# A Hedgehog-attention and MoE kernel: a new issue order with smaller first MoE blocks, 64-row tiles for the q products, and results on VectorE

One core of a Trainium2 chip. The metric is device time in microseconds (us) of one execution, the median over several.

## The reference

Linear attention with a learned feature map, then a layer norm and a two-layer channel network ("MoE") with a residual. Shapes: 8 batches, 8 heads, 576 tokens, 64 columns per head; model width 512, hidden width 2048.

```python
def phi(x):                                    # x: (8, 8, 576, 64)
    proj = einsum('bhsd,df->bhsf', x, w_phi)   # f = 128
    proj = proj - max(abs(proj), axis=-1, keepdims=True)
    return concatenate([exp(proj), exp(-proj)], axis=-1)
q_p, k_p = phi(q), phi(k)
kv  = einsum('bhsf,bhsd->bhfd', k_p, v);  z = sum(k_p, axis=2)
att = einsum('bhsf,bhfd->bhsd', q_p, kv) / (einsum('bhsf,bhf->bhs', q_p, z)[..., None] + 1e-06)
x   = att.transpose(0, 2, 1, 3).reshape(8, 576, 512)
xn  = (x - mean(x)) / sqrt(var(x) + 1e-06) * g_ln
out = x + maximum(xn @ w_ch1, 0.0) @ w_ch2
```

## The kernel before

It works on pairs of batches. A "unit" is two sequences of 576 tokens (one head of both batches of a pair; in the first pair, two heads of one batch), so there are 32 units. Each operation is registered with an engine, an estimated duration, a rank and what it reads and writes; a list scheduler in the source then fixes one order of instructions per engine. Each engine gets its instructions in that order; the traces below show instructions held up behind one that waits (3.53 us on ScalarE in the first new dent). From unit 8 on q and k are cast to bf16 by any of three engines and transposed by DMA, before that on TensorE. Fillers are matmuls on zeros, meant to keep TensorE's clock up.

In the profile lines PE is TensorE (PEld its weight loads), DVE VectorE, ACT ScalarE, POOL GpSimd and SPq the queue that issues most DMAs. A timeline line gives start and duration in us; brackets hold the engine's idle time before it and what ended that.

```python
DUE = 24.7; BLOCK = 127.5; WARM = 45.0
...
b16_bufs = [consts.tile([P, ST], BF16, name=f"b16_{i}") for i in range(2)]   # cast q, k
...
def a_trans_dma(u):
    b16 = b16_bufs[n % 2]            # cast (DVE, ACT or GpSimd) -> b16 -> DMA transpose -> qkT
...
def a_main(u, i):                    # i = 0: q, i = 1: k
    for c in range(4):               # full rows, a zero-padded block weight: two heads at once
        nc.tensor.matmul(ps[:, 2 * c : 2 * c + 2, :],
            u["qkT"][:, (i * 4 + c) * P : (i * 4 + c + 1) * P], wbk, start=True, stop=True)
...
def a_tails(u):                      # q products, transposed
    for i in range(2):
        nc.tensor.matmul(ps[:, i * 512 : (i + 1) * 512], wbk[:, i, :], u["qkT"][:, 0:512],
                         start=True, stop=True)
...
# MoE: blocks of three token tiles (384 columns) for xn @ w_ch1, then 512 columns per tile for w_ch2
def result(engine):                  # (DVE, ACT): on ACT in 26 of 36 cases
    nc.scalar.activation(o, ch[t], AF.Copy, scale=pr["rstd"][:, t : t + 1])
def residual():
    nc.gpsimd.tensor_tensor(out=ch["o", t], in0=ch["o", t], in1=x[:, t, :], op=ALU.add)
```

## Time and profile before

| | before |
|---|---|
| time, median of 3 | 389.92 us (389.59 to 390.96) |
| span of the profiled run | 388.8 us |
| TensorE busy | 364.6 us, 94% |
| first MoE matmul | 49.13 us |
| last matmul ends, then tail | 382.8 us, 6.0 us |

"Busy" here includes fillers and waits inside a pipelined group, so the share says little. The prediction below shows the lines and turns them into a ledger of useful and lost TensorE time.

### The profile page before, as it was taken

How to read it: one execution, taken by the hardware profiler on the slowest of the kernel's cores; microseconds unless marked ns; L12 is line 12 of the kernel's file. 1: busy time of each engine (PE TensorE's matmuls, PEld its weight loads, DVE VectorE, ACT ScalarE, POOL GpSimd, SP SyncE). 2: the span in 40 equal slices, each digit the busy share in tenths (PEclk: the TensorE clock that was granted, in tenths of full speed). 3: DMA queues.
4: the chain of work that ended last, by engine and by line, in shares of the span. 5: the costliest groups of instructions: out<-in, count | busy, mean ns of one | idle time of the engine just before them, and what ended most of it. 6: DMA issues, size and time to landing. Idle time of an engine off the chain costs nothing.

```text
span 388.8 us, 8917 instructions
## 1 busy us (share of the span) xinstructions
PE 364.6 (94%) x3307; PEld 232.5 (60%) x3354; DVE 255.0 (66%) x556; ACT 259.8 (67%) x576; POOL 201.9 (52%) x348
## 2 busy tenths in 40 slices
PE   3999995999999989999999999999999999999993
PEld 1888864666766554666666556666665555555541
DVE  3788995899999999997897998696757000000000
ACT  2877885899786857797976887686946444444411
POOL 3667987577576836664936655935841111111022
PEclk9999998799999999999999999999999999999998
DMA  7999889979799284948861486220007030110012
GB/s 208 300 227 279 262 150 170 222 189 254 197 245 232 64 230 111 236 129 190 183 186 36 124 163 157 57 60 2 30 27 137 31 90 29 27 56 27 30 66 71
DMA packets 92444, 53.28 MB, mean 137 GB/s; under 512 B 58992, under 2 KB 87792, under 8 KB 92400
## 3 DMA queue, kind: packets, MB, share of 16 engines
q1 hardware_dynamic: 86400, 47.79, 48.8%
q0 software_dynamic: 4224, 4.19, 6.9%
q10 hardware_dynamic: 1776, 0.72, 0.7%
q8 instruction: 26, 0.43, 0.5%
q14 instruction: 18, 0.15, 0.1%
HBM read 36.77 MB, written 9.44 MB: 119 GB/s over the span
## 4 chain that ended last, share of the span: by engine, by line
PE 57%; issue 21%; DVE 11%; DMA 6%; POOL 3%; ACT 1%; POOLq 0%; SPq 0%; DVEq 0%
PE hT_ps L1006 20%; PE ch_ps L1037 16%; PE pm L624 6%; DMA qkT_130<-b_0_131 4%; PE n_bank L734 3%; POOL o L1056 3%; PE num L780 3%; PE n_bank L1215 2%; PE pt L699 2%; DVE m_137 L631 1%; DVE m_135 L631 1%; DMA qx_106<-in_k_dram 1%; DVE w_120 L451 1%; DVE st_147 L933 1%; PE n_bank L729 1%
## 5 line engine op out<-in xcount | busy, mean ns | idle before, releaser
L1037 PE MATMUL ch_ps<-w_121,hT 128*128 128x512 bf16 x541 | 145.3, 379 | 1.6
L1006 PEld LDWEIGHTS <-w_120 128*128 128x128 bf16 x768 | 72.7, 98 | 55.9 <-issue 2.5
L1016 ACT ACTIVATE hT<-hT_ps 128x384 bf16<-128x384 f32 x113 | 55.6, 493 | 59.4 <-PE hT_ps L1006 58.9
L1037 PEld LDWEIGHTS <-hT 128*128 128x128 bf16 x576 | 53.3, 98 | 43.8
L820 POOL TENSOR_TENSOR x<-numc,rden 128x384 bf16<-128x384 f32 (+3 forms) x88 | 46.2, 541 | 62.4 <-DVE rden L814 58.2
L1056 POOL TENSOR_TENSOR o<-o,x 128x512 f32<-128x512 f32 x26 | 30.1, 1157 | 85.9 <-ACT o L1050 80.5
L1006 PE MATMUL hT_ps<-xT_127,w_120 128*128 128x384 bf16 x256 | 52.0, 326 | 0.1
L1006 PE MATMUL hT_ps<-xT_125,w_120 128*128 128x384 bf16 x256 | 50.2, 329 | 1.4 <-DVE hT L1014 0.9
L1006 PE MATMUL hT_ps<-xT_126,w_120 128*128 128x384 bf16 x256 | 51.2, 326 | 0.1
L1014 DVE TENSOR_SCALAR hT<-hT_ps 128x384 bf16<-128x384 f32 x79 | 42.9, 549 | 9.8 <-PE hT_ps L1006 9.2
L643 ACT ACTIVATE eb_134<-pm 128x1024 bf16<-128x1024 f32 x32 | 32.8, 1036 | 3.5 <-DVE m_137 L631 1.5
L643 ACT ACTIVATE eb_133<-pm 128x1024 bf16<-128x1024 f32 x32 | 31.7, 1025 | 4.9 <-DVE m_137 L631 3.8
L705 ACT ACTIVATE ea_118<-pt 128x1024 bf16<-128x1024 f32 x32 | 31.9, 1032 | 4.0 <-PE pt L699 2.4
L705 ACT ACTIVATE ea_116<-pt 128x1024 bf16<-128x1024 f32 x32 | 31.5, 1028 | 4.2 <-PE num L786 1.5
L631 DVE TENSOR_REDUCE m_136<-pm 128x8 f32<-128x1024 f32 x22 | 26.6, 1215 | 6.4 <-PE pm L624 6.3
L631 DVE TENSOR_REDUCE m_135<-pm 128x8 f32<-128x1024 f32 x22 | 26.7, 1215 | 4.0 <-PE pm L624 4.0
L1045 DVE SCALAR_TENSOR_TENSOR o<-ch_ps,rstd_157,x 128x512 f32<-128x512 f32 x2 | 1.5, 752 | 41.4 <-PE ch_ps L1037 41.4
L631 DVE TENSOR_REDUCE m_137<-pm 128x8 f32<-128x1024 f32 x20 | 24.3, 1214 | 2.1 <-PE pm L624 2.1
L1215 PE MATMUL n_bank<-wz 128*128 128x120 bf16 x301 | 22.4, 221 | 1.6 <-DVE KV L742 1.0
L804 DVE TENSOR_TENSOR numc<-num,em 128x390 f32<-128x390 f32 (+1 forms) x40 | 20.3, 515 | 4.6 <-PE num L780 4.4
L810 DVE TENSOR_TENSOR numc<-numc,num 128x390 f32<-128x390 f32 (+1 forms) x40 | 20.4, 515 | 0.7
L1215 PEld LDWEIGHTS <-wz 128*128 128x128 bf16 x301 | 18.6, 101 | 3.1 <-issue 2.1
(204 smaller groups left out, 649.5 us busy)
## 6 DMA issues: line engine op xcount, KB each, us to landing
out_dram<-o SPq DMA_DIRECT2D x32, 256.0 KB, 2.5
qk_100<-in_k_dram SPq DMA_DIRECT2D x12, 256.0 KB, 3.8
v_101<-in_v_dram SPq DMA_DIRECT2D x12, 256.0 KB, 3.7
qk_102<-in_k_dram SPq DMA_DIRECT2D x10, 256.0 KB, 3.4
qk_102<-in_q_dram SPq DMA_DIRECT2D x10, 256.0 KB, 4.1
v_103<-in_v_dram SPq DMA_DIRECT2D x10, 256.0 KB, 4.6
qk_104<-in_k_dram SPq DMA_DIRECT2D x10, 256.0 KB, 4.0
qk_104<-in_q_dram SPq DMA_DIRECT2D x10, 256.0 KB, 4.7
```

What stands on the lines that cost most here:

```text
L624: nc.tensor.matmul(ps[:, 2 * c : 2 * c + 2, :], u["qkT"][:, (i * 4 + c) * P : (i * 4 + c + 1) * P], wbk, start=True, stop=True,)
L631: nc.vector.reduce_max(out=u["m"][:, i, 0:MX], in_=u["pm", i], axis=AX.X, apply_absolute_value=True)
L643: nc.scalar.activation(u["EB"][:, t, 0:MX, :], u["pm", 1], AF.Exp, scale=(1.0, -1.0)[t])
L705: nc.scalar.activation(u["EA"][:, t, 0:1024], u["pt"], AF.Exp, scale=(1.0, -1.0)[t])
L810: nc.vector.tensor_add(out=st["numc"], in0=st["numc"], in1=st["ps"][0])
L820: nc.gpsimd.tensor_tensor(out=dst, in0=st["numc"][ps_, i : i + n, 0:D], in1=bcast(st["rden"][ps_, i : i + n], 2, D), op=ALU.mult,)
L1006: nc.tensor.matmul(st["ps"], w1_sb[:, kc, jj * P : (jj + 1) * P], xT_bufs[(pair * NR + r) % XB][:, kc::KC, :], start=(kc == 0), stop=(kc = ...
L1014: nc.vector.tensor_relu(h_sb, st["ps"])
L1016: nc.scalar.activation(h_sb, st["ps"], AF.Relu)
L1037: nc.tensor.matmul(ch[t], hT[r, jj][:, rt * P : (rt + 1) * P], w2_sb[:, jj, :], start=(jj == 0), stop=(jj == JC - 1),)
L1056: nc.gpsimd.tensor_tensor(out=ch["o", t], in0=ch["o", t], in1=x[:, t, :], op=ALU.add)
L1215: nc.tensor.matmul(warm, wz, wz[:, 0:WN], start=False, stop=False, skip_group_check=True)
```

## The change

The intent: start the MoE sooner, so that fillers give way to useful work; halve the cost of q's products; shorten the tail; model the DMA rings in the scheduler so that no transposed data comes late. The scheduler and the ranks are rewritten, and with them every engine's order. The core, cut:

```diff
-DUE = 24.7
-BLOCK = 127.5
-WARM = 45.0
+DUE, SLOPE = 33.0, 1.3
+WARM = 36.0
+OFF = ( {"en": 0, "gln": 404.4, "k": 731.6, ... "mixed": 18.6, ...}, ... )   # new ranks [cut]
...
+    # MoE blocks in token tiles: the first pair of batches in 2, 2, 2 and 3, the others in 3
+    BLOCKS = (((0, 2), (2, 4), (4, 6), (6, 9)), *(((0, 3), (3, 6), (6, 9)),) * (NPAIR - 1))
...
+    # units 0 to 3: k and v of four units are loaded first, q is done in two halves (s = 0, 1) [cut]
...
+    def a_qt(u):                                # units 4 to 31: q and transposed q in one group
+        rows = [slice(a * D, (a + 1) * D) for a in range(2)]
+        for c in range(4):
+            for a in range(2):
+                nc.tensor.matmul(pq[:, a, c, :], qT[rows[a], c * P : (c + 1) * P],
+                                 wst[rows[a], :], start=True, stop=True)
+        for a in range(2):
+            nc.tensor.matmul(pt[:, a * 512 : (a + 1) * 512], wst[rows[a], :],
+                             qT[rows[a], 0:512], start=True, stop=True)
...
-            def result(engine):   # DVE, or ACT with the residual on GpSimd
+            def result():
+                nc.vector.scalar_tensor_tensor(
+                    out=o[:, cols], in0=ch[t, c][:, cols], scalar=pr["rstd"][:, t : t + 1],
+                    in1=x[:, t, cols], op0=ALU.mult, op1=ALU.add)   # the last tile in two halves
```

What it leaves alone matters too: there are still two cast buffers (`b16_bufs`).

## The prediction

> **What bounds the kernel now.** I read the page's shares first, then the busy table by stretches of the span, then TensorE's timeline, the chain of waits, and TensorE's groups by shape. TensorE is busy 94% of the span; nothing else passes 67%. The question is how much of that is useful.
>
> ```profile
> PE 364.6 (94%) x3307; PEld 232.5 (60%) x3354; DVE 255.0 (66%) x556; ACT 259.8 (67%) x576; POOL 201.9 (52%) x348
> PE   3999995999999989999999999999999999999993
> PEclk9999998799999999999999999999999999999998
> ```
>
> The tenths show a slow start, one dent near slices 6 and 7 (60 to 75 us) with a lower clock, and a full row from there to the end. The table (stretch in us, then mean length, busy us of PE, PEld, DVE, ACT, POOL, clock, DMA) sizes the parts:
>
> ```profile
> 5.00:10.00 5.00, 2.56 (x13) 1.27 (x14) 2.57 (x5) 2.57 (x4) 0.00 (x0) 1.00 1.08 290
> 60.00:70.00 10.00, 5.76 (x67) 4.05 (x68) 5.99 (x12) 4.92 (x8) 5.59 (x16) 0.77 1.26 188
> 120.00:140.00 20.00, 18.18 (x166) 11.13 (x168) 19.69 (x37) 14.30 (x31) 12.30 (x19) 1.00 0.65 180
> 320.00:340.00 20.00, 19.89 (x108) 10.59 (x109) 0.75 (x1) 8.92 (x18) 2.31 (x2) 1.00 0.09 27
> ```
>
> Up to 49 us TensorE is "busy" with fillers: matmuls on a zero tile that only keep its clock up. The first MoE matmul (L1006) starts at 49.13. The dent is a wait for one transposing DMA, issued at 52.16 and landed 15.38 us later, while the second weight's four loads (issued from 51.05 on) are in the rings:
>
> ```profile
> L1215 PE MATMUL n_bank<-wz 128*128 128x120 bf16 x301 | 22.4, 221 | 1.6 <-DVE KV L742 1.0 <-ACT KV L744 0.5
> 49.13 0.81 PE L1006 MATMUL hT_ps<-xT_125,w_120 128*128 128x384 bf16 x4
> 51.05 2.30 POOL L435 DMA_DIRECT2D w_121<-in_moe_w_ch_dram  x3
> 52.16 15.38 DMA qkT_130<-b_0_131
> 67.59 1.03 PE L624 MATMUL pm<-wbk,qkT_130 128*128 128x256 bf16 x4 [3.71 <-DMA qkT_130<-b_0_131]
> ```
>
> Durations of overlapped matmuls are no cost, so I take the distance between starts. 16 matmuls of 384 columns stand in the chain as 2.60 us, 0.1625 each; 9 of 512 columns as 1.94, 0.2157 each. The MoE is 768 and 576 of these (541 of the latter are recorded): 124.8 + 124.2 = 249.0 us. One attention unit, from the starts in the timeline: key products 0.44 (35.03 to 35.47), query products 0.44, transposed query products 0.43 (61.58 to 62.01), mixed tail 0.16, kv 2 x 0.31, numerators 0.37 + 0.25: 2.71 us, times 32 = 86.7. Transposes of the first eight units 8 x 0.5 = 4, of x 36 x 0.056 = 2. **Useful work: 341.7 us.** The last matmul ends near 382.8, so 41 us of TensorE's time is lost. A ledger by stretch finds it: fillers 301 at 0.053 to 0.107, about 17.5; idle in the first 10 us 6.5; half clock for useful work until 13 us, about 2.5; idle from 10 to 50 us 1.9; from 50 to 70 us 5.2; half clock after the dent about 2; idle from 70 to 160 us 3.0; from 160 to 380 us 1.6. Sum 40.2. So the time is useful work, plus what is lost before and around the MoE's start, plus a tail:
>
> ```profile
> 382.91 0.69 ACT L1050 ACTIVATE o<-ch_ps,rstd_157 128x512 f32<-128x512 f32 x1 [2.81 <-PE ch_ps L1037]
> 383.68 1.15 POOL L1056 TENSOR_TENSOR o<-o,x 128x512 f32<-128x512 f32 x1 [2.35 <-ACT o L1050]
> 384.86 1.12 SPq L987 DMA_DIRECT2D out_dram<-o  x2
> ```
>
> The tail is 382.8 to 388.8: 6.0 us. The reported time is 1.1 above the span.
>
> **What the Trainium skill says.** (1) "TensorE: Matmul & The Clock Gate", Part 1: a TensorE left idle for a window of about 3.4 us drops to half its clock and needs as much activity to return. The trace agrees: after 3.71 us of idle the key products show 414 ns each instead of 272. (2) "TensorEngine Tiling (Array Packing)", Theoretical Speedup and Key Properties: contracting 64 rows or fewer allows two row tiles side by side, up to 2x, and changing the tiling mode drains the engine. No matmul of the kernel before is tiled, so its trace shows neither; the query products do have 64 useful rows against a zero-padded 128-row weight. (3) The same page, Gotcha 1: row tiles must not write one PSUM bank at the same time; the new code gives each its own 512 columns of f32. (4) "DMA: Bandwidth & Descriptors", Queues, rings and completion order: each DMA engine takes turns between rings by packets. The 15.4 us landing beside the weight loads, against 3.2 to 5.3 us medians for these transposes, fits that.
>
> **The change, part by part.**
> *Start.* The first MoE block shrinks from three token tiles to two, whose attention needs only half of q, and loads put k and v of four units first. Before, tiles of all four units' q preceded it. The bound is now a chain through GpSimd: scaled v of unit 0 can start near 10 us (first key-tail work is at 8.4 before, em at 10.7); four units at two times 1.5 us is 12 us, weight issues 4 x 0.85 = 3.4, early puts 6 x 0.36 = 2.2: 27 us. Then kv, its copy, numerators, division and puts, about 3.5 us, and statistics, centring, transposes and copies, about 3: 33.5. ACT needs only 4 x (1.9 + 1.0 + 0.65 + 0.6) = 17 us by then and fits. The order was made by a model, and queues slip against it, so I take 36 us, 13 before today's 49. The first MoE weight was issued at 14.4 to 16.8 and took at most 17.9 us, hence by about 35: not later than needed, but without much to spare. Fillers now start at 1.3 instead of 10.5 us, so the first useful products should meet a full clock: 2.5 us less.
> Of the 26 us from 10 to 36, useful work takes about 11.5 (four units at 0.44 + 0.16 + 0.62 + half of 0.87 and 0.37 = 1.85; transposes 2.5; a little of the next ones); 14.5 remain filler or idle, against 27 or so in the 39 us today. Blocks 0 and 1 hold 4/36 of 249 = 27.7 us of MoE and the rest of units 0 to 7 some 14 us, so 42 us of work is there from 36 us on, while DVE and ACT need about 18 + 7.5 = 26 us for units 4 to 7: TensorE need not starve.
> *The dent.* Second-weight loads come earlier, and DMA turns are modelled; I take away most of the 5.2 + 2 us and leave bubbles of 5.5 us in all from 36 us on, where today (after 50) they are 11.8.
> *64-row tiles.* 28 of 32 units: eight 128-column products in pairs, 4 x 0.056 = 0.22 for 0.44, and 0.22 for 0.43; less two mode changes, for which the source's own model has 0.095 each: 0.87 - 0.44 - 0.19 = 0.24 us, times 28 = 6.6 us, all on the bound engine.
> *Results on DVE.* 26 results leave ACT (0.69) and GpSimd (1.15) for one DVE operation of 0.75: +19.5 us on DVE, -18 on ACT. Relus can move to ACT. On the path only the tail counts: 0.69 + 1.15 become 0.4 to 0.75, on a half-width last piece: the tail goes from 6.0 to about 4.
> Sum: useful 341.7 - 6.6 = 335.1; lost 6.5 - 1 (idle early) + 14.5 + 5.5 = 25.5, rounded up to 26.5 for a later MoE start; tail 4; 1.1 for span to time: 366.7. I put 368, as a new order usually brings a wait of its own.
>
> **Rivals.** (a) DVE becomes the bound between 40 and 160 us: it already shows 19.69 of 20 us there, and the results add to it. For it: PE loses 1.8 us in just that stretch. Against: ACT has 5.7 us free in it, and later DVE is idle. Were it so, another 6 to 10 us of bubbles: 374 to 378. (b) The DMA rings hold the early MoE: about 9 MB must have landed by 36 us and 12 MB by 50, and today's rings move 12.5 MB by 50. Then MoE starts at 40 or stalls again at the second weight, with a cold clock: 373 to 380. (c) Row tiles do not run side by side, or the drain costs as much as it saves; each unit holds both wide PSUM tiles at once: 6 to 9 us lost, 375. (d) Everything lands as planned at 33.5 us: 363.
>
> **Range and chances.** One rival in full costs about 7 us, two about 14, so 360 to 378 should hold 8 times in 10. The limit of 2% is 382: it takes three rivals together. Faster 0.94, same 0.05, slower 0.01.
>
> **What would show it.** Right: first L1006-like matmul near 36 us; fillers from 1.3 us at the low end; no wait over 2 us on a transposing DMA and clock 1.00 after 10 us; pairs of query products that start nearly together, groups of 0.6 us where they were 0.87; a tail near 4 us. Wrong: a first MoE matmul after 42 us, TensorE under 9 tenths between 40 and 160 us with DVE full, a second dent in the clock, or a tiled group that takes as long as the old one.

## The result, and the profile after

| | before | after |
|---|---|---|
| time, median of 4 | 390.08 us (389.59 to 390.96) | 383.89 us (383.05 to 385.29) |
| ratio, 95% interval | | 0.9844 (0.9800 to 0.9888): the same at 2% |
| span, mean clock | 388.8 us | 381.3 us, 0.993 |
| first MoE matmul | 49.13 us | 46.33 us |
| fillers recorded | 301 | 309 |
| last matmul ends, then tail | 382.8 us, 6.0 us | 377.4 us, 3.9 us |

Ratios here and below are the mean time of one kernel's fast runs over the mean of the other's fast runs of the same rounds, so they are not quite the ratio of the medians quoted. All runs in this study were in the fast state (none over 1.5% above the fastest of its kernel). A difference between two variants in us is the difference of their ratios times 390.3.

The change gained 6.2 us where 22 had been predicted. The page after (tenths of TensorE, fillers):

```profile
PE   7999689996997999999999999999999999999995
L1347 PE MATMUL n_bank<-wz 128*128 128x120 bf16 x309 | 23.0, 223 | 0.4 <-DVE KV L850 0.4
```

The old dent at 60 to 75 us is gone, but slices 5, 10 and 13 (of 9.5 us each: from 38, 86 and 114 us on) are new ones. The table by stretches, in the columns that the prediction names; a dent costs more than its idle time, as the granted clock (third figure from the end) is 0.86 from 90 to 100 us:

```profile
60.00:70.00 10.00, 10.00 (x125) 7.49 (x120) 9.31 (x20) 6.91 (x18) 8.07 (x15) 1.00 0.91 183
80.00:90.00 10.00, 6.52 (x75) 4.05 (x73) 6.28 (x17) 6.47 (x17) 4.87 (x10) 0.97 1.17 225
90.00:100.00 10.00, 10.00 (x108) 6.59 (x107) 8.64 (x20) 8.62 (x23) 6.12 (x10) 0.86 1.06 261
120.00:140.00 20.00, 16.71 (x181) 10.38 (x181) 19.97 (x38) 13.14 (x31) 15.67 (x25) 1.00 0.84 224
```

To see where time was won and lost I counted the useful matmuls begun by a given moment, each at the full-clock distance between starts that the prediction derives (fillers at zero, a 64-row group at the cost of the full-row one that it replaces). Differences under 1 us mean nothing:

| useful TensorE work by | 49 us | 60 | 80 | 100 | 120 |
|---|---|---|---|---|---|
| before | 19.5 | 28.6 | 41.7 | 61.6 | 81.4 |
| after | 22.5 | 30.6 | 50.4 | 65.4 | 85.1 |
| lead of after | 3.0 | 2.0 | 8.7 | 3.8 | 3.7 |

The trace of the change has all its matmuls. That of the kernel before lacks 35 of the 576 for w_ch2 and 12 of the 64 transposed q products, 10 us of work over the whole span. With these filled in by the order of experiment 8, whose records are complete, the leads are 2.3, 2.3, 8.3, 3.6 and 3.5 us.

So the start brought 2 to 3 us; the missing old dent another 6 to 7; and between 80 and 100 us 5 of them are lost again.

**The late start.** The first MoE matmul, and the waits just ahead of it:

```profile
45.06 0.22 PE L838 MATMUL n_bank<-vv,eb 128*128 128x130 bf16 x1 [1.09 <-POOL vv L668]
45.38 0.38 PE L997 MATMUL xT_ps<-ident,xc 128*128 128x128 bf16 x4
...
46.33 1.03 PE L1120 MATMUL hT_ps<-xT,w 128*128 128x256 bf16 x8 [0.31 <-ACT xT L1009]
```

The first block needs scaled v (`vv`) of four units from GpSimd, as the prediction's chain had it. But GpSimd, busy until 21.4 us, then stands:

```profile
23.26 0.75 POOL L917 TENSOR_TENSOR x<-numc,rden 128x128 bf16<-128x128 f32 x2 [1.81 <-DVE rden L911]
...
29.51 1.71 POOL L917 TENSOR_TENSOR x<-numc,rden 128x128 bf16<-128x128 f32 x5 [3.29 <-DVE rden L911]
31.66 1.05 POOL L659 TENSOR_TENSOR vv<-v,em 128x512 bf16<-128x512 f32 x1
```

The puts (L917) are at the head of its queue and wait 6.55 us in all (1.81, 1.45 and 3.29) for divisions on DVE; the fourth unit's scaled v is queued behind them. It is done at 34.7 us. My sum had added GpSimd's busy times, 27 us, as if nothing in its queue waited. From there to the start it is 11.6 us, where the sum had 6.5. The fence above shows a part of this: in TensorE's queue a product of the sixth unit stands ahead of the second half of x's transposes (L997), and it waits 1.09 us for GpSimd.

**The new dents.** The first, near 85 us:

```profile
80.49 5.68 SPq L568 DMA_TRANSPOSE qkT<-b  x2
87.35 1.04 ACT L547 CAST b<-qk 128x1024 bf16<-128x1024 f32 x1 [3.53 <-DMA qkT<-b]
88.30 0.83 ACT L1009 ACTIVATE xT<-xT_ps,ngln 128x256 bf16<-128x256 bf16 x2
88.82 0.59 PE L1150 MATMUL ch_ps<-w,hT 128*128 128x512 bf16 x2 [3.48 <-ACT xT L1009]
```

Read from below: TensorE waits 3.48 us for a copy of x's transposes on ACT (`xT`); that copy stands behind a cast of q and k into a buffer `b`; and the cast waits 3.53 us for a DMA to have read that buffer, a transposition from an earlier unit. TensorE doesn't need the cast data at that moment. In the dent of before it did: its own wait named the transposed data.

The second dent, near 120 us, begins in the same way on DVE and GpSimd (casts wait for a transposition, 0.53 and 2.50 us), and goes on with work on DVE, three weight scalings among it, ahead of a maximum that TensorE's next PSUM slot waits for:

```profile
116.23 1.92 DVE L545 CAST b<-qx 128x128 bf16<-128x128 f32 x1 [0.53 <-DMA qkT<-b]
118.07 2.49 DVE L467 TENSOR_SCALAR w<-w,gln 128x512 bf16<-128x512 bf16 x3
120.48 1.21 DVE L803 TENSOR_REDUCE m<-pq 128x8 f32<-128x1024 f32 x1
121.74 0.49 PE L632 MATMUL pk<-wbk,qkT 128*128 128x256 bf16 x3 [2.11 <-DVE m L803]
```

**The tiles**, a group of eight and two matmuls, between the starts of its neighbours:

```profile
204.87 0.81 PE L1120 MATMUL hT_ps<-xT,w 128*128 128x384 bf16 x4
205.61 0.40 PE L784 MATMUL pq<-wst,qkT 64*128 64x128 bf16 x8
205.85 0.38 PE L789 MATMUL pt<-qkT,wst 64*128 64x512 bf16 x2
206.16 0.23 PE L838 MATMUL n_bank<-vv,eb 128*128 128x130 bf16 x1
```

From 205.61 to 206.16 it is 0.55 us. The four matmuls before it (0.1625 each, from 204.87) should end at 205.52, so the change of mode takes 0.09 more on the way in: 0.64, against 0.88 on full rows (experiment 2). So do 27 of the 28 groups; the first, at 39.74, takes 0.69.

**The tail**, from the end of the last matmul (377.4) through a half-width result on DVE, and its store, to the span's end at 381.3: 3.9 us.

```profile
377.54 0.48 DVE L1157 SCALAR_TENSOR_TENSOR o<-ch_ps,rstd,x 128x256 f32<-128x256 f32 x1 [0.38 <-DMA out_dram<-o]
```

### The profile page after: what moved, and what is told of

It reads as the page before. It is cut to its first block, busy times and chain, and to the rows that moved or that the text cites. A ratio compares the mean times of both kernels' runs of the same rounds, so it can differ in the third digit from the quotient of the medians.

```text
span 381.3 us, 9349 instructions
## 1 busy us (share of the span) xinstructions
PE 361.3 (95%) x3562; PEld 230.4 (60%) x3562; DVE 296.8 (78%) x633; ACT 226.3 (59%) x539; POOL 181.5 (48%) x334
## 4 chain that ended last, share of the span: by engine, by line
PE 54%; POOL 1%; DMA 1%; DVE 0%; SPq 0%; issue 0%; DVEq 0%
PE ch_ps L1150 23%; PE hT_ps L1120 22%; PE n_bank L843 2%; PE num L887 1%; PE pk L632 1%; PE pq L784 1%; PE pt L789 1%; DMA out_dram<-o 1%; PE n_bank L838 1%; PE n_bank L887 1%; POOL vv L659 1%; PE n_bank L893 0%; PE n_bank L590 0%; DVE o L1157 0%; POOL vv L668 0%; POOL vv L664 0%
## 5 line engine op out<-in xcount | busy, mean ns | idle before, releaser
L1150 PE MATMUL ch_ps<-w,hT 128*128 128x512 bf16 (+1 forms) x592 | 153.3, 375 | 3.5 <-ACT xT L1009 3.5
L1120 PE MATMUL hT_ps<-xT,w 128*128 128x384 bf16 (+1 forms) x832 | 153.9, 315 | 0.8 <-ACT xT L1009 0.3
L1120 PEld LDWEIGHTS <-w 128*128 128x128 bf16 x832 | 77.6, 98 | 54.0 <-issue 4.6
L1128 DVE TENSOR_SCALAR hT<-hT_ps 128x384 bf16<-128x384 f32 (+1 forms) x136 | 71.3, 525 | 49.4 <-PE hT_ps L1120 47.5
L659 POOL TENSOR_TENSOR vv<-v,em 128x512 bf16<-128x512 f32 x64 | 67.1, 1049 | 23.7 <-ACT em L645 14.9
L917 POOL TENSOR_TENSOR x<-numc,rden 128x384 bf16<-128x384 f32 (+3 forms) x88 | 45.8, 534 | 66.0 <-DVE rden L911 64.0
L1130 ACT ACTIVATE hT<-hT_ps 128x384 bf16<-128x384 f32 (+1 forms) x72 | 33.3, 465 | 66.9 <-PE hT_ps L1120 66.5
L648 ACT ACTIVATE eb<-pk 128x1024 bf16<-128x1024 f32 x64 | 65.7, 1043 | 5.4 <-DVE m L638 5.3
L810 ACT ACTIVATE ea<-pt 128x1024 bf16<-128x1024 f32 x56 | 57.0, 1028 | 15.9 <-PE pt L789 15.4
L638 DVE TENSOR_REDUCE m<-pk 128x8 f32<-128x1024 f32 x32 | 38.8, 1213 | 5.0 <-PE pk L632 4.9
L803 DVE TENSOR_REDUCE m<-pq 128x8 f32<-128x1024 f32 x28 | 33.9, 1210 | 1.0 <-PE pq L784 1.0
L843 PEld LDWEIGHTS <-eb 128*128 128x128 bf16 x512 | 22.3, 98 | 7.0 <-issue 4.1
```

The lines of the kernel that those rows point to most:

```text
L638: nc.vector.reduce_max(out=u["m"][:, 1, 0:MX], in_=u["pk"], axis=AX.X, apply_absolute_value=True)
L648: nc.scalar.activation(u["EB"][:, t, 0:MX, :], u["pk"], AF.Exp, scale=(1.0, -1.0)[t])
L659: nc.gpsimd.tensor_tensor(out=u["vv"][:, t, 0:MX, 0:D], in0=vb[:, hh, :].rearrange("p (c d) -> p c d", d=D), in1=bcast(e[:, 0:MX], 2, D), ...
L803: nc.vector.reduce_max(out=out, in_=ps, axis=AX.X, apply_absolute_value=True)
L810: nc.scalar.activation(u["EA"][:, t, :], u["pt", None], AF.Exp, scale=(1.0, -1.0)[t])
L843: nc.tensor.matmul(ps[:, t, c // 4, :], EB[:, t, c, :], vv[:, t, c, :], start=False, stop=(t == 0 and c == MX - 1), skip_group_check=True,)
```

## The experiments

Fifteen kernels ran, all timed in five rounds against the kernel before; all but the last three (wrong on purpose) gave the right result. "Order unchanged" means that every engine's sequence is that of the change but for the edit itself. My theory after reading the result: the new dents come from the two cast buffers. The rivals: DVE's load makes them; the tiles or the results cost more than they bring; the MoE simply starts too late.

**1. The change again**, as the control of its call.

> The changed kernel unaltered, as the control of this call: 0.984 of the kernel before (it had 383.9 against 390.1 us), last matmul near 377, an idle of 3.5 us of TensorE at 84 us and one of about 2 us at 119 us. If the idle times are not in this profile again, they are accidents of one run and the theories built on them fall.

384.77 us (382.31 to 385.06), ratio 0.9841 (0.9811 to 0.9870). Both dents were there again (idle 2.84 us from 85.4 on, 3.57 from 118.9 on). They are not an accident of one run.

**2. Tiles undone**, order unchanged:

```diff
-    pq[:, a, c, :], qT[rows[a], c * P : (c + 1) * P], wst[rows[a], :],
+    pq[:, a, c, :], qT[:, c * P : (c + 1) * P], wbk[:, a, :],
-    pt[:, a * 512 : (a + 1) * 512], wst[rows[a], :], qT[rows[a], 0:512],
+    pt[:, a * 512 : (a + 1) * 512], wbk[:, a, :], qT[:, 0:512],
```

> Same order of instructions, same PSUM layout; only the query products of 28 units use the zero-padded 128-row weight (eight 128-column products one after the other, two 512-column ones) instead of 64-row tiles. Theory A (tiles pay as predicted): TensorE's groups grow from about 0.65 to 0.87 us, 28 x 0.22 = 6.2 us of a bound engine, so 5 to 6.5 us slower than the control. Rival B (the drain eats it, or the time lies elsewhere): within 2 us of the control.

388.23 us, ratio 0.9949 (0.9921 to 0.9976): 4.2 us slower than the control. The group, from 207.81 to the next start at 208.69, takes 0.88:

```profile
207.81 0.61 PE L784 MATMUL pq<-wbk,qkT 128*128 128x128 bf16 x8
208.26 0.59 PE L789 MATMUL pt<-qkT,wbk 128*128 128x512 bf16 x2
208.69 0.22 PE L838 MATMUL n_bank<-vv,eb 128*128 128x130 bf16 x1
```

All 28 groups take that. So the tiles save (0.878 - 0.641) x 28 = 6.6 us in the groups, but only 4.2 us of time, give or take 1.6 (the two intervals combined). The rest comes back as waits: from the first MoE matmul to the last matmul TensorE is idle for 9.0 us with the tiles and for 6.8 without.

**3. Four cast buffers**, order unchanged (five buffers for hidden activations given up for the room):

```diff
-    b16_bufs = [... for i in range(2)]        b16 = b16_bufs[n % 2]        # hT: bufs=HB (34)
+    b16_bufs = [... for i in range(4)]        b16 = b16_bufs[n % 4]        # hT: bufs=29
```

> Same order; four buffers instead of two for the cast data that the transposing DMAs read (the relu tiles get 29 buffers instead of 34 to make room; the planned order never needs over 27). Theory A (the idle at 84 us is ACT, in order, held by a cast that waits for a transposing DMA to release its buffer): the 3.5 us idle and its 1.5 us of half clock go, 3 to 5 us faster than the control. Rival B (the DMA rings are late and TensorE needs the transposed data itself): the idle stays or moves by a unit, within 1.5 us.

377.54 us (376.79 to 379.67), ratio 0.9682 (0.9653 to 0.9712): 6.2 us faster than the control. The transpositions still take 5.5 us to be issued, but the cast no longer waits for them, and TensorE's wait falls from 3.48 to 0.18:

```profile
80.31 5.48 SPq L568 DMA_TRANSPOSE qkT<-b  x2
84.40 1.05 ACT L547 CAST b<-qk 128x1024 bf16<-128x1024 f32 x1 [0.24 <-DMA qk<-in_q_dram]
85.87 0.59 PE L1150 MATMUL ch_ps<-w,hT 128*128 128x512 bf16 x2 [0.18 <-ACT xT L1009]
```

In the change casts waited 13.0 us on GpSimd and 7.7 on ACT for these transpositions over the whole run; here none does. Between 80 and 90 us TensorE is busy 9.81 of 10 us, where it was 6.52, and the granted clock is 1.00 from 80 to 100. In the place of the second dent no wait is longer than 0.74 us (at 124). By 120 us this version has done 88.7 us of useful work against the change's 85.1. The buffers are the cause of the dents, and slow transpositions alone are not.

**4. The 16 weight scalings from DVE to ACT**, two buffers, order unchanged:

```diff
-    nc.vector.tensor_scalar(out=w1_sb[:, kc, sl], in0=w1_sb[:, kc, sl], scalar1=gln_sb[...], scalar2=-1.0, ...)
+    nc.scalar.activation(w1_sb[:, kc, sl], w1_sb[:, kc, sl], AF.Copy, scale=ngln[:, kc : kc + 1])
```

> Same order; the 16 scalings of the first weight go to ACT instead of DVE. Theory A (DVE is the bound from 116 to 140 us: 99% busy, the scalings take 0.6 us there for a planned 0.3, and each of the three idles of TensorE follows a group of them): the idles at 119, 130 and 138 us (3.6 us) go, 2.5 to 4.5 us faster. Rival B (the bound there is the whole attention chain, or ACT becomes it): within 1.5 us.

383.60 us, ratio 0.9835 (0.9803 to 0.9867): no different from the control. In the worst stretch for DVE its busy time falls from 19.97 us to 13.80, ACT's rises from 13.14 to 18.61, and TensorE's doesn't move (16.71, now 16.54):

```profile
120.00:140.00 20.00, 16.54 (x170) 10.09 (x170) 13.80 (x28) 18.61 (x42) 15.73 (x26) 1.00 0.99 236
```

The second dent's wait of 2.11 us is gone, but others took its place: 1.12 us for a load of q at 130, 1.39 behind a copy on ACT at 139. A full DVE was not what cost time with two buffers, at least not in a way that moving its load to ACT cures.

**5. Four buffers without the tiles** (edits 2 and 3).

> The version with four cast buffers, with the query products on full rows again. In the version with two buffers the tiles were worth only 4.2 us of a predicted 6.2. Theory A (the rest was hidden under the idle times that wait for other things): here, with fewer of them, 5.5 to 6.5 us slower than with tiles, about 0.984 of the kernel before. Rival B (a tile saves only 0.15 us a unit): again about 4 us, 0.979.

382.44 us, ratio 0.9806 (0.9781 to 0.9830): 4.8 us slower than four buffers with tiles. So the tiles are worth 4 to 5 us in either version. With an interval of some 1.5 us either way this doesn't decide between the two expectations; the trace does: a group takes 0.64 us here too, so a tile saves 0.24 a unit, and not 0.15.

**6. Four buffers and an earlier MoE start**: one rank changed, and the scheduler, which still reckons with two buffers, makes a new order from it.

```diff
-    "mixed": 18.6,
+    "mixed": -900,
```

> Four cast buffers, and a rank that lets the fourth unit's mixed product have a PSUM slot at once instead of 11 us later; the order is planned anew, with the first MoE product some 5 us earlier (41 instead of 46 us). Theory A (of the prediction: an earlier MoE start is worth its time one to one): 3 to 5 us faster than four buffers alone, 0.957. Rival B (TensorE's supply between 46 and 90 us is bound by the attention that feeds the later blocks, so an earlier start only moves the idle): within 2 us, or slower, 0.968 to 0.985.

387.57 us, ratio 0.9935 (0.9915 to 0.9954): 10 us slower than four buffers with the order unchanged, though the MoE starts at 41.3 us instead of 46.6. It is ahead at first (useful work by 80 us: 52.5 against 50.2) and behind at 160 us (118.4 against 127.5). A miss for my theory that the late start costs its length. From the first MoE matmul on TensorE is idle for 11.3 us, against 4.4 with the order unchanged, and the granted clock falls to 0.83 from 80 to 100 us and 0.93 from 140 to 160, where it was 1.00; that is 3.4 and 1.4 us of full clock:

```profile
80.00:100.00 20.00, 17.34 (x178) 11.42 (x175) 17.82 (x40) 15.22 (x39) 15.00 (x24) 0.83 1.03 238
```

No wait before the first fall, near 93 us, is longer than 0.81 us; several short ones come close together there. The prediction's first point from the skill speaks of a TensorE left idle for about 3.4 us; here the clock fell without such a wait.

**7. Four buffers, results back on ACT and GpSimd**, 27 of 37, order unchanged:

```diff
+    if pair < NPAIR - 1:
+        nc.scalar.activation(o, ch[t, c], AF.Copy, scale=pr["rstd"][:, t : t + 1])
+        nc.gpsimd.tensor_tensor(out=o, in0=o, in1=x[:, t, :], op=ALU.add)
+        return
     nc.vector.scalar_tensor_tensor(...)
```

> Four cast buffers; 27 of the 37 results (all but the last pair's) go back to ACT plus GpSimd, at the same place in the order. Theory A (results on DVE cost time where DVE is full, 40 to 160 us): 2 to 4 us faster. Rival B (DVE, ACT and GpSimd are all near full there and in order, so the work only changes sides): within 1.5 us or slower by up to 3, since GpSimd takes 1.15 us and feeds the kv products.

382.29 us, ratio 0.9803 (0.9777 to 0.9828): 4.7 us slower, more than either theory had allowed. Results on DVE help in this order, where the other engines' queues were made without them; TensorE then waits for scaled v behind the residual adds (1.32 us until 76.0, 1.22 until 246.6).

**8. The kernel before with 64-row tiles alone**:

```diff
+    if i == 0 and n >= 4:                       # q products in pairs of 64-row tiles
+        for c in range(4):
+            for a in range(2):
+                nc.tensor.matmul(ps[:, 4 * a + c, :], qkT[rows(a), c * P : (c + 1) * P], wst[rows(a), :], ...)
...                                              # and the transposed q products likewise [cut]
```

> The kernel before with 64-row tiles for the query products of units 4 to 31 and nothing else, in its own order. Theory A (tiles pay on their own, 28 x 0.22 us): 5 to 6.5 us faster than the kernel before, 0.985, as much as the whole change gained. Rival B (they pay only in the new order, or DVE and ACT limit the stretches): under 3 us, above 0.992.

390.48 us, ratio 1.0004 (0.9986 to 1.0021): no gain. There the two halves are separate groups between full-row work, and each pays the change of mode by itself:

```profile
202.48 0.81 PE L1055 MATMUL ch_ps<-w,hT 128*128 128x512 bf16 x3
203.22 0.40 PE L629 MATMUL pm<-wst,qkT 64*128 64x128 bf16 x8
203.55 0.50 PE L1024 MATMUL hT_ps<-xT,w 128*128 128x384 bf16 x2
```

Three matmuls of 0.2157 should end the first group at 203.13; the tiled one starts 0.09 later and lasts 0.33 to the next: 0.42, against 0.44 on full rows. The median of the 28 groups is 0.42 too, and that of the 28 transposed ones 0.42 against 0.43. Putting both q products into one group is what makes the tiles pay.

**9 and 10. Two other orders of the same program** as the change with four cast buffers, from a search over the ranks, by a scheduler that knows of the four buffers and takes 0.5 us for a weight scaling instead of 0.3: one planned to start the MoE early, one late, with the same planned end.

```diff
-OFF = ( {"en": 0, "gln": 404.4, "k": 731.6, ...}, ... )
+OFF = ( {"en": 13.4, "gln": 126.6, "k": -37.3, ...}, ... )     # order_early
+OFF = ( {"en": 0, "gln": -421.4, "k": 170.1, ...}, ... )       # order_late
```

> Four cast buffers known to the planner, 0.5 us planned for a weight scaling, ranks searched anew; of several searched orders with the same planned end this is the one with the earliest MoE start (planned 39.6 us, 4 us before the changed kernel's 43.8). Theory A (an earlier MoE start is worth its time): 4 us or more faster than its partner order_late, near 0.955. Rival B (the start is not the bound, the attention behind it is): within 1.5 us of the partner.

> The partner: same code, searched ranks with the same planned end, MoE planned to start at 45.7 us, 6 us after order_early. Theory A: 4 us or more slower than order_early. Rival B: within 1.5 us. Both orders should be near the version with four buffers in the changed order (377.5 us, 0.968) if an order of equal plan is equal on the chip.

order_early 383.64 us, ratio 0.9834 (0.9807 to 0.9861); order_late 383.00 us, ratio 0.9804 (0.9774 to 0.9834). Their first MoE matmuls came at 42.3 and 49.0 us (the last figures ahead of the form are the first and last start):

```profile
L1099 PE MATMUL hT_ps<-xT,w x832: 269/326/525, 42.3 to 366.3; 128*128 128x384 bf16 x128, 128*128 128x256 bf16 x39
```
```profile
L1099 PE MATMUL hT_ps<-xT,w x832: 270/326/422, 49.0 to 364.2; 128*128 128x384 bf16 x128, 128*128 128x256 bf16 x39
```

By 60 us the early one has 34.3 us of useful work done against 31.6, by 120 us 83.9 against 83.4: the lead has been used up. (Both traces lack some 40 of the matmuls for w_ch2, so this is good to 1 or 2 us.) And both are some 5 us slower than the change's own order with four buffers, which starts in between. An order that looks as good in the plan need not be as good on the chip.

**11. The kernel before with four cast buffers** (edit 3 on it).

> The kernel before with four cast buffers instead of two, same order. Theory A (its dent at 63.8 us has the cause of the new one, a cast held in order behind a transposing DMA): the 3.7 us idle and the 2 us of half clock go, 4 to 5.5 us faster, 0.987. Rival B (there TensorE itself waits for transposed data that land 15 us after their issue): the dent stays, within 1.5 us.

390.76 us, ratio 0.9999 (0.9978 to 1.0019): no gain. The old dent stays: TensorE itself waits for transposed data, whose transposition, issued at 52.12 us, landed 16.11 us later; the next one took 7.09 us to be issued.

```profile
52.12 16.11 DMA qkT<-b
59.85 7.09 SPq L560 DMA_TRANSPOSE qkT<-b  x1
68.28 1.03 PE L624 MATMUL pm<-wbk,qkT 128*128 128x256 bf16 x4 [5.12 <-DMA qkT<-b]
```

**12. Four buffers, every second scaling on ACT** (edits 3 and 4, `if kc % 2`), order unchanged.

> Four cast buffers in the changed order, every second weight scaling on ACT. Moving all 16 (with two buffers) freed DVE from 19.0 to 13.8 of 20 us and filled ACT to 18.6, for no gain. Theory A (balanced halves do what all of them could not): the three idles of 0.7 to 0.9 us after 120 us go, 1.5 to 2.5 us faster than four buffers alone, 0.963. Rival B (in order, a scaling delays whatever stands behind it on either engine): within 1 us.

375.28 us (375.01 to 380.24), ratio 0.9636 (0.9595 to 0.9677), right result: the best version of this study, 14.9 us under the kernel before and 1.8 us under experiment 3, though the two were in different calls and their intervals overlap.

**13 to 15. No scalings at all**, wrong results on purpose: the two searched orders and the change with four buffers. If DVE's load eats the early lead, relief should help the early order more than the late one.

```diff
-    nc.vector.tensor_scalar(out=w1_sb[:, kc, sl], in0=w1_sb[:, kc, sl], ...)
+    pass
```

> Wrong result on purpose: the order with the early MoE start (order_early, 383.6 us, first MoE product at 42.3 us), with the 16 scalings of the first weight left out and nothing put in their place; everything else in the same order. That takes 16 times about 0.6 = some 10 us of work off DVE between 40 and 145 us. Theory 'DVE eats the lead' (the early lead of about 2 us of useful work at 60 us is lost to 120 because DVE is over 90% busy from 40 to 160 us): then the early start keeps its lead once DVE is relieved: 375 to 377 us, and 3 us or more better than the late order with the same relief. Theory 'the order's own waits, not DVE's load': 381 to 384 us, no better than the late order.

> Wrong result on purpose: the partner order with the late start (order_late, 383.0 us, first MoE product at 49.0 us), with the 16 scalings left out in the same way. Theory 'DVE eats the lead': 379 to 381 us, so 3 us or more behind the early order with the same relief. Theory 'own waits': within 1.5 us of the early order, whichever time both take.

> Wrong result on purpose: the order of the change with four cast buffers (377.5 us), the 16 scalings left out. Bounds what the scalings cost on the path in the order of the change. Theory 'DVE's load': 372 to 374 us, as half of them moved to ACT gave 2 us. Theory 'waits': 375 to 377 us, no more than the version with half of them on ACT (375.3).

383.25 us, ratio 0.9834 (0.9802 to 0.9866); 382.87 us, ratio 0.9824 (0.9787 to 0.9862); and 374.18 us, ratio 0.9595 (0.9562 to 0.9628). Some 10 us of DVE work less bring the early order nothing, the late one nothing, and the change's order 3.4 us. So the lead is not lost to DVE's load, but to waits of the order itself. One is plain in the early order, near 107 us:

```profile
104.91 1.89 POOL L528 TENSOR_TENSOR b<-qk,one 128x1024 bf16<-128x1024 f32 x1 [3.17 <-DMA qk<-in_q_dram]
104.97 2.38 DVE L524 CAST b<-qk 128x1024 bf16<-128x1024 f32 x1 [2.61 <-DMA qk<-in_q_dram]
107.72 0.28 ACT L582 ACTIVATE eb<-n_bank 128x128 bf16<-128x128 f32 x1 [3.16 <-DVE m L573]
108.56 0.27 PE L866 MATMUL n_bank<-KV,ea 128*128 128x65 bf16 x2 [3.06 <-ACT ex L586]
```

DVE and GpSimd stand with casts at the head of their queues whose q has not been loaded; ACT waits for a maximum behind the cast on DVE, and TensorE for ACT. Without the scalings the same wait is there (2.30 us of TensorE at 109.96, behind the cast that waits for the load of q). It is the pattern of the new dents once more, with a load in place of a buffer.

## Why the prediction was wrong

The direction and the mechanism of several parts were right; the time came out 16 us longer than foretold. By the prediction's own terms, in us of gain; its ledger had 28.4 us lost up to 50 us (17.5 + 6.5 + 2.5 + 1.9) and 11.8 from there on:

| term | predicted | measured | how measured |
|---|---|---|---|
| up to the MoE's start | 28.4 to 21.0: 7.4 | 2.3 | lead in useful work at 49 us, missing records filled in |
| bubbles afterwards | 11.8 to 5.5: 6.3 | -3.5 | the rest of the 5.4 us by which the last matmul ends sooner |
| 64-row tiles | 6.6 | 6.6 | 28 groups, 0.64 for 0.88 us |
| tail | 2.0 | 2.1 | 6.0 to 3.9 |
| sum | 22.3 | 7.5 | the spans, 388.8 and 381.3 |

The first two are good to about 1 us.

**"I take away most of the 5.2 + 2 us and leave bubbles of 5.5 us in all from 36 us on"** is the step that failed by most, 10 us: the bubbles did not shrink to 5.5 us but grew to some 15. Its first half was right: the old dent went (by 80 us the lead is 8.7 us). Its second half was a guess without a mechanism. I counted the work available to TensorE and the load of DVE and ACT, found enough of the one and not too much of the other, and concluded that "TensorE need not starve". I didn't ask what each in-order queue has at its head, and what that waits for. Two cast buffers cost the old order nothing (experiment 11); in the new one the casts run into them. Experiment 3 gives back 6.2 of the 10 us, and shows the chain broken.

**"I take 36 us, 13 before today's 49"**: 46.33. The chain through GpSimd was the right one, but its length was summed from busy times, and the puts in it wait on DVE: scaled v of four units came at 34.7 us, not at 27, and the rest took 11.6 us, not 6.5. (The scheduler's own plan, says the expectation of order_early, had the start at 43.8 us.) The prediction also took the 14.5 us of fillers and idle as the remainder up to 36; with a start 10 us later the fillers stayed (309 for 301). Whether the whole loss of 5.1 us in this row comes from the late start is another matter. Two pairs of orders say that the start's moment is worth little by itself: with a start at 41.3 us the kernel was 10 us slower than with 46.6 (experiment 6), and with 42.3 no better than with 49.0, with DVE's scalings (9, 10) and without (13, 14). An early lead came up against later waits each time. These orders differ in much more than the start, so it is shown that an earlier start didn't help in these, not that it can't. That step treated filler time as a cost which an early start removes; it is only removed if all that follows keeps up.

**"0.87 - 0.44 - 0.19 = 0.24 us, times 28 = 6.6 us"**: right in mechanism and size, 0.878 - 0.641 = 0.24 a group. What it left out is that some 2 us of this come back as waits: the time gained 4.2 us (experiment 2) and 4.8 (5). The grouping of both products, which the prediction took for granted, is what makes it positive (experiment 8).

**The tail**: right within 0.1 us. **Fillers from 1.3 us**: they came at 1.39, and up to 20 us of the span the lead in useful work was about 1 us (6.7 against 5.7), less than the 2.5 us expected of the clock alone.

**The rivals.** (a) DVE as the bound: its load was as foretold (19.97 of 20 us at 120 to 140), but the verdict on it is mixed. Shifting the load with two buffers gave nothing (experiment 4); with four it gave 1.8 us, and leaving it out altogether 3.4 (12, 15). It was not the main cause of the miss. (b) DMA: half right. The MoE did start after 40 us, but behind GpSimd and DVE, not behind the rings; there was a second stall behind slow transpositions, reached by way of a buffer and not of the data. (c) Tiles: no; they ran as fast as predicted, and only the waits took back a third of their gain. The prediction gave each rival about 7 us, said that the limit of 2% "takes three rivals together", and took that for unlikely. They are not independent: all are ways for a dense new order to run into a wait, and a piece of (a) and of (b) came.

What stays open: why the change's own order, with four buffers, beats two others of equal plan by 5 us. One wait of 3 us in the early one is shown, and in the late one the granted clock was 0.83 from 40 to 60 us (1.00 in the change's order with four buffers), which is 3.4 us of full clock; the rest is spread over waits of 1.5 us or less, which I didn't trace one by one. Open too are the 3 to 4 us between the bubbles that four buffers leave and the 5.5 predicted.

## What to carry to other kernels

Busy shares and sums of busy times don't say how an in-order queue will run: for each engine on the path, ask what stands at the head of its queue and what that instruction waits for, buffers being refilled by a slow DMA above all. When a reordering moves work earlier, count the buffers between producers and a slow transfer again; here two more small buffers were worth as much as the whole change. And a model that plans an order can be wrong by more than the gains it is chosen for, so time several orders on the chip.

## What the Trainium skill lacked or had wrong

- "TensorEngine Tiling (Array Packing)", Key Properties, says that a change of tiling mode drains the engine, without a figure. Here it cost about 0.09 us on the way in, and a lone group of eight 64x128 matmuls took 0.42 us against 0.44 on full rows (no gain, 1.0004), where ten matmuls in one group took 0.64 against 0.88. The page's "up to 2x" needs that beside it.
- "DMA: Bandwidth & Descriptors" gives no figure for how long the queue that issues transposing DMAs is held beside other traffic; it only has sequencer cycle counts, in a comparison of a later chip with the generations before it. Here one took 1.28 us at its shortest, two beside loads 5.48 to 5.68, and one in experiment 11 7.09; in the first new dent the cast that reuses the source buffer waited 3.53 us.
- "GPSIMD Engine Reference", Specifications, says that GpSimd shares its SBUF interfaces with VectorE, which contends in some modes. The skill says more of this elsewhere, so it is no gap; the runs add numbers. This trace agrees: of three 128x128 casts on VectorE the shortest took 0.18 us and the longest 1.92, beside a 1.89 us multiplication on GpSimd that ended with it, and the weight scalings ranged from 0.32 to 1.13 us. A model with one duration each is off by that.
